# A two-matmul GELU block on one core: the first product wholly in half-row passes, ahead of the second product

## The chip, the core and the metric

The kernel runs on one core of one Trainium2 chip. The metric is device time in microseconds, the median of several runs. The profile used here is one profiled execution of the same kernel on the same kind of chip; all times in it are microseconds from the start of its span unless marked ns.

## The reference

```python
B, S, D, F = 1, 2048, 448, 1792          # all bf16
def reference(x, w1, b1, w2, b2):
    h = jnp.einsum("bsd,df->bsf", x, w1) + b1
    h = _gelu(h)                          # tanh approximation
    return jnp.einsum("bsf,fd->bsd", h, w2) + b2
```

## The kernel before

The 2048 rows of `x` are taken in four chunks of 512 (`SC`), the 1792 hidden columns in 14 tiles of 128 (`NFT`). A "tile" of the first product is one pair (chunk c, hidden tile ft): 128 hidden columns by 512 rows, accumulated in one PSUM bank. There are 56, in the list `order`, and eight banks (`ps`, `NB`).

The contraction of the first product has 448 rows, which is three and a half times 128. `KROW = [0, 128, 256, 320]` cuts both operands into four row blocks; blocks 2 and 3 overlap by 64 rows. A tile is made of three *full* matmuls of 128 rows (`full`, L229) and one *half* matmul of 64 rows (`half`, L237), which uses either the lower or the upper 64 rows of the array. Even tiles take blocks 0, 1, 2 in full and the upper half of block 3; odd tiles take blocks 0, 1, 3 in full and the lower half of block 2 (`SLOTS`, `HALVES`). The halves of two neighbouring tiles use different row halves of the array and so run side by side.

Changing between full and half form is grouped by blocks of eight tiles (`BLOCK`, `FIRST`): the `first` tiles of a block run their full matmuls, then their halves; the `second` tiles begin with their halves and end with their full matmuls. So each of the seven blocks changes form twice. The first block, `opening_block`, goes by row blocks instead of by tiles, because the row blocks of w1 land one after the other (semaphores `sem_w10`, `sem_w1`, and `sem_w1r` for the columns from tile 8 on).

Before the first matmul, 13 dummy matmuls run (L200). Chunk 0 of `x` is loaded in its natural layout and transposed by 16 matmuls with an identity (L214) in six parts (`XPARTS`); each part lies in a bank of its own from `XBANK` on, and VectorE (`d`, L352) or ScalarE (`a`, L336) copies it to `xT_sb`. The bias `b1` is transposed by one small matmul (L205) among them and copied by VectorE (L354). The other three chunks are transposed by their loads (`load_xT`, L164, four transposing DMAs a chunk).

ScalarE evicts each finished tile with GELU and bias (L340) into `g_sb`, in `order`. The second product (`l2`, L317) takes the 128-row stripes of a chunk: 14 matmuls of 448 columns each accumulate in one bank, VectorE adds `b2` (L358), and SP stores the stripe (L183). The last stripe is cut in two column parts.

TensorE's order is the list `schedule`: blocks of the first product, with the second product of a chunk put in as soon as the chunk after it is through the first (chunk 0 after block 3, chunk 1 after block 5, chunks 2 and 3 at the end). `jobs` numbers all bank uses in that order, a bank is taken in turn, and `free` waits until the use eight before has been evicted. SP's queue has the loads in this order: `x` chunk 0, w1, the transposing loads of chunk 1, w2, b2, the transposing loads of chunks 2 and 3, then the stores.

Of the kernel before, what the change touches and what calls it, by code (L numbers as in the profile page):

```python
# [11 lines left out]
def bass_standalone__dense_activation_gelu__prompt_kernel(  # L12
# [10 lines left out]
    P = 128  # L23
    HALF = P // 2
# [17 lines left out]

    BLOCK = 8
    FIRST = [4] + [6] * 6
    W2_PIECES = [(0, 7), (7, 14)]


# [1 line left out]
        ("d", [(0, 0)]), ("a", [(0, 1)]), ("d", [(1, 0)]), ("a", [(1, 1)]),  # L53
        ("d", [(0, 2), (0, 3)]), ("a", [(1, 2), (1, 3)]),
    ]
    XBANK = 1
    NB = 8

    NWARM = 13
# [2 lines left out]
    OCUT = 256  # L62

    order = [(c, ft) for c in range(NSC) for ft in range(NFT)]
    BLOCKS = []
    for i, n in enumerate(FIRST):
        tiles = order[i * BLOCK:(i + 1) * BLOCK]
        BLOCKS.append((tiles[:n], tiles[n:]))
    assert len(BLOCKS) * BLOCK == len(order)

    schedule = []
    done = 0
    for i, (first, second) in enumerate(BLOCKS):
        schedule.append(("l1", i))
        while done < NSC - 2 and (done + 1, NFT - 1) in order[:(i + 1) * BLOCK]:
            schedule.append(("l2", done))
            done += 1
    schedule += [("l2", c) for c in range(done, NSC)]

    outs = [(j, 0, D) for j in range(NST - 1)] + [(NST - 1, 0, OCUT), (NST - 1, OCUT, D)]  # L80

    jobs = []
    for what, c in schedule:
        if what == "l1":
            jobs += [("g", order.index(tile)) for part in BLOCKS[c] for tile in part]
        else:
            jobs += [("o", n) for n, (j, _, _) in enumerate(outs) if j // STC == c]
    number = {job: n for n, job in enumerate(jobs)}  # L90

    with ExitStack() as es:
# [27 lines left out]
        sem_b1T = S_("sem_b1T")  # L120
        sem_b1 = S_("sem_b1")
        sem_l1 = S_("sem_l1")
        sem_g = S_("sem_g")
        sem_l2 = S_("sem_l2")
        sem_osb = S_("sem_osb")
# [11 lines left out]
        def x_part(n, parts):  # L137
            h, k = parts[0]
            to = xT_sb[:, k:k + len(parts), 2 * h * P:2 * (h + 1) * P]
            src = ps[XBANK + n][:, 0:2 * P * len(parts)]  # L140
            return to, src.rearrange("p (k t) -> p k t", k=len(parts))

        def load_w1(eng):
# [26 lines left out]
        @block.sync  # L170
        def _(sp):
            sp.dma_start(xn_sb[:, 0:2, :], x0_view[:, 0:2, :]).then_inc(sem_xn[0], 16)  # L172
            sp.dma_start(xn_sb[:, 2:4, :], x0_view[:, 2:4, :]).then_inc(sem_xn[1], 16)  # L173
            load_w1(sp)
            load_xT(sp, 1)
            for i in range(len(W2_PIECES)):
                load_w2(sp, i)
            sp.dma_start(b2_bc[:, :], b2.partition_broadcast(P)).then_inc(sem_b2, 16)
            for c in range(2, NSC):
                load_xT(sp, c)  # L180
            for j in range(NST - 1):
                sp.wait_ge(sem_osb, j + 1)
                sp.dma_start(out_dram(j), out_sb[:, j, :]).then_inc(sem_od, 16)  # L183
            sp.wait_ge(sem_od, 16 * NST)
# [11 lines left out]
        def _(pe):  # L196
            ones_w = nc.const_aps.tensor(1.0, [P, P], BF16)
            ones_x = nc.const_aps.tensor(1.0, [P, WN], BF16)
            for _i in range(NWARM):
                pe.matmul(ps[0][:, 0:WN], lhsT=ones_w, rhs=ones_x, start=True, stop=True)  # L200
            pe.wait_ge(sem_id, 2)
            for n, (_, parts) in enumerate(XPARTS):
                if n == 2:
                    pe.wait_ge(sem_b1n, 16)
                    pe.matmul(  # L205
                        ps[NB - 1][:, 0:NFT], lhsT=b1n_sb[:, :], rhs=ident[0:NFT, 0:NFT],
                        start=True, stop=True,
                    ).then_inc(sem_b1T, 1)
                for h, k in parts:
                    if (h, k) in ((0, 0), (1, 0)):  # L210
                        pe.wait_ge(sem_xn[h], 16)
                    for t in range(2):
                        col = parts.index((h, k)) * 2 * P + t * P
                        mm = pe.matmul(  # L214
                            ps[XBANK + n][:, col:col + P],
                            lhsT=xn_sb[:, 2 * h + t, KROW[k]:KROW[k] + P],
                            rhs=ident[:, :],
                            start=True, stop=True,
                        )
                mm.then_inc(sem_xtp, 1)  # L220
# [4 lines left out]
                    kind, i = jobs[n]  # L225
                    pe.wait_ge(sem_g if kind == "g" else sem_osb, i + 1)

            def full(c, ft, k, start, stop):
                return pe.matmul(  # L229
                    bank("g", order.index((c, ft)))[:, :],  # L230
                    lhsT=w1_sb[:, k, ft * P:(ft + 1) * P],
                    rhs=xT_sb[:, k, c * SC:(c + 1) * SC],
                    start=start, stop=stop,
                )

            def half(c, ft, k, lo, start, stop):
                return pe.matmul(  # L237
                    bank("g", order.index((c, ft)))[:, :],
                    lhsT=w1_sb[lo:lo + HALF, k, ft * P:(ft + 1) * P],
                    rhs=xT_sb[lo:lo + HALF, k, c * SC:(c + 1) * SC],  # L240
                    start=start, stop=stop,
                )

            SLOTS = ((0, 1, 2), (0, 1, 3))
            HALVES = ((3, HALF), (2, 0))

            def opening_block(first, second):
                first = [ft for _, ft in first]
                second = [ft for _, ft in second]

                fts = first + second
                for n, ft in enumerate(fts):
                    for i, (a, _) in enumerate(W0_PIECES):
                        if ft == a:
                            pe.wait_ge(sem_w10[i], 16)
                    if n == 0:
                        pe.wait_ge(sem_xTd, 2)
                    elif n == NB - 1:
                        pe.wait_ge(sem_b1, 1)
                    elif XPARTS[n - XBANK][0] == "a":  # L260
                        pe.wait_ge(sem_xTa, sum(e == "a" for e, _ in XPARTS[:n - XBANK + 1]))
                    elif n - XBANK >= 4:
                        pe.wait_ge(sem_xTd, sum(e == "d" for e, _ in XPARTS[:n - XBANK + 1]))
                    full(0, ft, 0, True, False)
                pe.wait_ge(sem_w1[1], 16)
                for n, ft in enumerate(fts):
                    full(0, ft, 1, False, False)
                pe.wait_ge(sem_w1[2], 16)
                pe.wait_ge(sem_w1[3], 16)
                for n, ft in enumerate(first):  # L270
                    full(0, ft, SLOTS[n % 2][2], False, False)
                for n, ft in enumerate(first):
                    half(0, ft, *HALVES[n % 2], False, True).then_inc(sem_l1, 1)
                for n, ft in enumerate(second):
                    half(0, ft, *HALVES[n % 2], False, False)
                for n, ft in enumerate(second):
                    full(0, ft, SLOTS[n % 2][2], False, True).then_inc(sem_l1, 1)

            def block_of(first, second):
                for n, (c, ft) in enumerate(first):  # L280
                    if c > 0 and ft == 0:
                        pe.wait_ge(sem_x[c], 16 * NKT)
                    free("g", order.index((c, ft)))
                    for k in SLOTS[n % 2]:
                        full(c, ft, k, k == 0, False)
                for n, (c, ft) in enumerate(first):
                    half(c, ft, *HALVES[n % 2], False, True).then_inc(sem_l1, 1)
                for n, (c, ft) in enumerate(second):
                    if c > 0 and ft == 0:
                        pe.wait_ge(sem_x[c], 16 * NKT)  # L290
                    free("g", order.index((c, ft)))
                for n, (c, ft) in enumerate(second):
                    half(c, ft, *HALVES[n % 2], True, False)
                for n, (c, ft) in enumerate(second):
                    for k in SLOTS[n % 2]:
                        mm = full(c, ft, k, False, k == SLOTS[n % 2][-1])
                    mm.then_inc(sem_l1, 1)

            def l1(i):
                if i == 0:  # L300
                    opening_block(*BLOCKS[i])
                    pe.wait_ge(sem_w1r, 32)
                else:
                    block_of(*BLOCKS[i])

            def l2(c):
                pe.wait_ge(sem_g, NFT * (c + 1))
# [14 lines left out]
                        )  # L322
                    mm.then_inc(sem_l2, 1)

            for what, c in schedule:
                (l1 if what == "l1" else l2)(c)

        @block.scalar
        def _(act):
# [16 lines left out]

        @block.vector
        def _(dve):
            for n, (e, parts) in enumerate(XPARTS):
                if e == "d":  # L350
                    dve.wait_ge(sem_xtp, n + 1)
                    dve.tensor_copy(*x_part(n, parts)).then_inc(sem_xTd, 1)  # L352
            dve.wait_ge(sem_b1T, 1)
            dve.tensor_copy(b1_f[:, :], ps[NB - 1][:, 0:NFT]).then_inc(sem_b1, 1)  # L354
            dve.wait_ge(sem_b2, 16)
            for n, (j, c0, c1) in enumerate(outs):
                dve.wait_ge(sem_l2, n + 1)
# [32 lines left out]
```

## Time and profile before

| | us |
|---|---|
| median of 3 runs | 96.71 (96.46 to 96.75) |
| profiled execution | 96.25 |
| its span | 94.4 |
| TensorE matmuls busy (PE) | 90.5 |
| TensorE weight loads busy (PEld) | 43.8 |
| ScalarE busy (ACT) | 35.9 |
| VectorE busy (DVE) | 11.7 |

The granted clock of TensorE is 1.0 in every stage of the span. The span is the time from the first to the last instruction that the profile has; the profiled execution's own time is 1.85 us longer. Matmuls are pipelined: a matmul of 512 columns is shown with a duration of about 379 ns though the next may start long before it ends, so a pace is read from several matmuls in a row. In the lines, `PE ps L229 x24` in the chain of waits means 24 instructions of line 229 one after the other; `<-` names what ended the idle time before.

### The profile page before, as it was taken

The numbers are of one execution on the slowest core, as the hardware profiler recorded it, in microseconds if no ns is written. First come the engines' busy times: TensorE is split into PE (matmuls) and PEld (weight loads), VectorE is DVE, ScalarE is ACT, GpSimd is POOL, SyncE is SP. The second block draws the span as 40 slices with busy tenths as digits, with TensorE's granted clock in tenths as the row PEclk, the third lists the DMA queues.
The fourth block names the chain that finished last, engine by engine and source line by source line (L and its number), as shares of the span: only waits on it lengthen the run. The fifth ranks groups of instructions, "written<-read, shape, count | busy, mean of one in ns | idle before, by whom it ended". The sixth has DMA issues, their size and how long they took to land.

```text
span 94.4 us, 1159 instructions
## 1 busy us (share of the span) xinstructions
PE 90.5 (96%) x492; PEld 43.8 (46%) x492; DVE 11.7 (12%) x21; ACT 35.9 (38%) x61; POOL 0.7 (1%) x6
## 2 busy tenths in 40 slices
PE   6989999999999999999999999999999999999990
PEld 4724343443443555544344455554345555555670
DVE  0320000000000022220000001222000222222130
ACT  3520595985958910000793990000099000000000
POOL 2000000000000000000000000000000000000000
PEclk9999999999999999999999999999999999999999
DMA  1999999998520010011000001110000110011111
GB/s 36 275 312 280 192 225 350 301 74 166 111 56 0 0 49 28 27 49 49 3 0 0 0 0 49 49 53 24 28 0 0 49 48 16 33 49 56 49 49 49
DMA packets 12385, 7.50 MB, mean 79 GB/s; under 512 B 7004, under 2 KB 11996, under 8 KB 12380
## 3 DMA queue, kind: packets, MB, share of 16 engines
q1 hardware_dynamic: 12208, 7.31, 32.9%
q10 hardware_dynamic: 172, 0.12, 0.4%
q8 instruction: 4, 0.07, 0.3%
q14 instruction: 1, 0.01, 0.0%
HBM read 4.02 MB, written 1.84 MB: 62 GB/s over the span
## 4 chain that ended last, share of the span: by engine, by line
PE 90%; DMA 5%; SPq 2%; DVE 0%; issue 0%
PE ps L317 45%; PE ps L229 38%; PE ps L237 7%; DMA wi_sb<-in_w_dram 5%; SPq L146 1%; SPq L173 0%; SPq L172 0%; DVE out_sb L358 0%
## 5 line engine op out<-in xcount | busy, mean ns | idle before, releaser
L340 ACT ACTIVATE g_sb<-ps,bi_f 128x512 bf16<-128x512 f32 x56 | 33.1, 702 | 34.9 <-PE ps L237 34.9
L317 PE MATMUL ps<-wo_sb,g_sb 128*128 128x448 bf16 (+2 forms) x238 | 42.9, 341 | 0.0
L229 PE MATMUL ps<-xT_sb,wi_sb 128*128 128x512 bf16 x168 | 38.2, 380 | 0.6 <-DMA wi_sb<-in_w_dram 0.4
L317 PEld LDWEIGHTS ps<-wo_sb,g_sb 128*128 128x128 bf16 x238 | 23.1, 98 | 19.7
L229 PEld LDWEIGHTS ps<-xT_sb,wi_sb 128*128 128x128 bf16 x168 | 15.7, 98 | 21.8 <-issue 3.0
L358 DVE TENSOR_TENSOR out_sb<-ps,bo_bc 128x448 bf16<-128x448 f32 (+2 forms) x17 | 10.2, 597 | 76.8 <-PE ps L317 76.8
L237 PE MATMUL ps<-xT_sb,wi_sb 64*128 64x512 bf16 x56 | 7.3, 379 | 0.0
L237 PEld LDWEIGHTS ps<-xT_sb,wi_sb 64*128 64x128 bf16 x56 | 2.2, 94 | 4.6 <-issue 3.0
L200 PE MATMUL ps<-const-bfloat16-1.0 128*128 128x256 bf16 x13 | 2.9, 410 | 0.8 <-PEq L375 0.8
L200 PEld LDWEIGHTS ps<-const-bfloat16-1.0 128*128 128x128 bf16 x13 | 1.8, 140 | 1.5 <-issue 0.7
L352 DVE CAST xT_sb<-ps 128x256 bf16<-128x256 f32 (+1 forms) x3 | 1.4, 510 | 3.8 <-PE ps L214 3.8
L332 ACT ACT_TABLE_LOAD x1 | 1.3, 1283 | 1.4 <-PEq L375 1.4
L336 ACT CAST xT_sb<-ps 128x256 bf16<-128x256 f32 (+1 forms) x3 | 1.3, 443 | 1.1 <-PE ps L214 1.0
L214 PE MATMUL ps<-ident,xn_sb 128*128 128x128 bf16 x16 | 1.2, 220 | 0.0
L214 PEld LDWEIGHTS ps<-ident,xn_sb 128*128 128x128 bf16 x16 | 1.0, 98 | 0.2
L190 POOL TENSOR_SCALAR_AFFINE_SELECT ident<-ident 128x128 bf16<-128x128 bf16 x1 | 0.3, 292 | 0.2 <-POOL ident L188 0.2
L332 ACT ACTIVATE act_junk<-const-float32-0.0 128x8 bf16<-128x8 f32 x1 | 0.2, 208 | 0.0
L188 POOL MEMSET ident<- 128x128 bf16 x1 | 0.2, 204 | 0.3 <-POOLq L375 0.3
L205 PE MATMUL ps<-ident,bin_sb 14*128 14x14 bf16 x1 | 0.2, 177 | 0.0
L354 DVE COPY bi_f<-ps 128x14 f32<-128x14 f32 x1 | 0.2, 161 | 0.0
L205 PEld LDWEIGHTS ps<-ident,bin_sb 14*128 14x128 bf16 x1 | 0.1, 90 | 0.1
L375 POOL MEMSET const-bfloat16-1.0<- 128x1 bf16 x1 | 0.1, 102 | 0.0
(3 smaller groups left out, 0.3 us busy)
## 6 DMA issues: line engine op xcount, KB each, us to landing
out_dram<-out_sb SPq DMA_DIRECT2D x15, 112.0 KB, 1.7
wo_sb<-in_w_dram SPq DMA_DIRECT2D x2, 784.0 KB, 6.5
wi_sb<-in_w_dram SPq DMA_DIRECT2D x3, 256.0 KB, 4.8
wi_sb<-in_w_dram SPq DMA_DIRECT2D x1, 576.0 KB, 6.8
xn_sb<-in_x_dram SPq DMA_DIRECT2D x2, 224.0 KB, 2.6
wi_sb<-in_w_dram SPq DMA_DIRECT2D x2, 128.0 KB, 3.4
wi_sb<-in_w_dram SPq DMA_DIRECT2D x1, 192.0 KB, 6.9
xT_sb<-in_x_dram SPq DMA_TRANSPOSE x12, 5.0
```

The source lines that it names most:

```text
L146: eng.dma_start(w1_sb[:, 0, a * P:b * P], w1[0:P, a * P:b * P]).then_inc(sem_w10[i], 16)
L200: pe.matmul(ps[0][:, 0:WN], lhsT=ones_w, rhs=ones_x, start=True, stop=True)
L205: pe.matmul(ps[NB - 1][:, 0:NFT], lhsT=b1n_sb[:, :], rhs=ident[0:NFT, 0:NFT], start=True, stop=True,).then_inc(sem_b1T, 1)
L214: mm = pe.matmul(ps[XBANK + n][:, col:col + P], lhsT=xn_sb[:, 2 * h + t, KROW[k]:KROW[k] + P], rhs=ident[:, :], start=True, stop=True,)
L229: return pe.matmul(bank("g", order.index((c, ft)))[:, :], lhsT=w1_sb[:, k, ft * P:(ft + 1) * P], rhs=xT_sb[:, k, c * SC:(c + 1) * SC], sta ...
L237: return pe.matmul(bank("g", order.index((c, ft)))[:, :], lhsT=w1_sb[lo:lo + HALF, k, ft * P:(ft + 1) * P], rhs=xT_sb[lo:lo + HALF, k, c * ...
L317: mm = pe.matmul(bank("o", n)[:, 0:c1 - c0], lhsT=g_sb[:, ft, j * P:(j + 1) * P], rhs=w2_sb[:, ft, c0:c1], start=(ft == 0), stop=(ft == NF ...
L332: act.activation(act_junk[:, :], zero, ACT.Gelu_apprx_tanh)
L336: act.copy(*x_part(n, parts)).then_inc(sem_xTa, 1)
L340: act.activation(g_sb[:, ft, c * SC:(c + 1) * SC], bank("g", i)[:, :], ACT.Gelu_apprx_tanh, bias=b1_f[:, ft:ft + 1], scale=1.0,).then_inc( ...
L352: dve.tensor_copy(*x_part(n, parts)).then_inc(sem_xTd, 1)
L358: dve.tensor_tensor(out=out_sb[:, j, c0:c1], in0=bank("o", n)[:, 0:c1 - c0], in1=b2_bc[:, c0:c1], op=ALU.add,).then_inc(sem_osb, 1)
```

## The change

The full matmuls of the first product are gone. Every tile is made of half-row matmuls alone, always two side by side, one in the lower and one in the upper half of the array's rows, for two neighbouring tiles. Two tiles need fourteen half matmuls, that is seven such *steps*. `PHASES` gives them: in the four steps of phase 0 the lower rows serve tile i+1 and the upper rows tile i; in the three steps of phase 1 it is the other way round. The two tiles have different banks, and the bank that a row half writes changes with the phase. Between a phase and the next of the same two tiles, a step waits (`sem_turn`) until the last step of the earlier phase has finished. Outside the opening, steps go by four tiles (`QUAD`): phase 0 of two tiles, phase 0 of the next two, then phase 1 of each.

The opening (`OPEN`) has 27 steps of the first eight tiles in three parts, one for what needs row block 0 of w1 alone, one after row block 1 has landed, one after blocks 2 and 3. The 28th step is put behind the first phase of tiles 8 and 9.

All 56 tiles now come before the second product; `schedule` and the blocks are gone. On SP's queue the transposing loads of chunks 2 and 3 go ahead of w2 and b2. The small matmul of `b1` goes ahead of the transposes and uses bank 0, its copy goes to the head of VectorE's stream, and the six transposed parts lie in banks 1, 2, 3, 4, 6 and 7.

```diff
-    BLOCK = 8
-    FIRST = [4] + [6] * 6
+    PHASES = (((0, 0), (1, 1), (2, 2), (3, 3)), ((0, 0), (1, 1), (2, 3)))
+    OPEN = (
+        ((0, 0, 0), (1, 0, 0), (2, 0, 0), (0, 1, 0), (1, 1, 0), (3, 0, 0), (2, 1, 0)),
+        ((0, 1, 1), (1, 1, 1), (3, 1, 0), (2, 1, 1), (0, 0, 1), (1, 0, 1), (3, 1, 1)),
+        ((0, 0, 2), (0, 0, 3), (1, 0, 2), (1, 0, 3), (0, 1, 2), (2, 0, 1), (1, 1, 2), (2, 0, 2),
+         (2, 0, 3), (3, 0, 1), (3, 0, 2), (3, 0, 3), (2, 1, 2)),
+    )
+    OPENING = 8
+    QUAD = 4
...
-    XBANK = 1
+    XBANK = [1, 2, 3, 4, 6, 7]
...
-    BLOCKS = []
...
-    schedule += [("l2", c) for c in range(done, NSC)]
+    steps = [(2 * j, h, m) for part in OPEN for j, h, m in part]
+    N_OPEN = [sum(len(part) for part in OPEN[:n]) for n in range(len(OPEN) + 1)]
+    def phase(i, h):
+        return [(i, h, m) for m in range(len(PHASES[h]))]
+    for i in range(OPENING, len(order), QUAD):
+        steps += phase(i, 0)
+        if i == OPENING:
+            steps.append((OPENING - 2, 1, len(PHASES[1]) - 1))
+        steps += phase(i + 2, 0) + phase(i, 1) + phase(i + 2, 1)
+    ahead = {}
+    turn = []
+    for n, (i, h, m) in enumerate(steps):
+        before = ahead.get(i)
+        turn.append(before if before is not None and steps[before][1] != h else None)
+        ahead[i] = n
+    turned = sorted(n for n in turn if n is not None)
...
+    jobs = [("g", i) for i in range(len(order))] + [("o", n) for n in range(len(outs))]
...
             load_xT(sp, 1)
+            for c in range(2, NSC):
+                load_xT(sp, c)
             for i in range(len(W2_PIECES)):
                 load_w2(sp, i)
             sp.dma_start(b2_bc[:, :], b2.partition_broadcast(P)).then_inc(sem_b2, 16)
-            for c in range(2, NSC):
-                load_xT(sp, c)
...
             pe.wait_ge(sem_id, 2)
+            pe.wait_ge(sem_b1n, 16)
+            pe.matmul(
+                ps[0][:, 0:NFT], lhsT=b1n_sb[:, :], rhs=ident[0:NFT, 0:NFT], start=True, stop=True,
+            ).then_inc(sem_b1T, 1)
...
+            def opening_waits(n, i):
+                if n == N_OPEN[1]:
+                    pe.wait_ge(sem_w1[1], 16)
+                if n == N_OPEN[2]:
+                    pe.wait_ge(sem_w1[2], 16)
+                    pe.wait_ge(sem_w1[3], 16)
+                if n < N_OPEN[1] and steps[n][1] == 0:
+                    for p, (a, _) in enumerate(W0_PIECES):
+                        if i == a:
+                            pe.wait_ge(sem_w10[p], 16)
+                    for t in (i, i + 1):
+                        if t == 0:
+                            pe.wait_ge(sem_b1, 1)
+                            pe.wait_ge(sem_xTd, 2)
...
+            def l1():
+                for n, (i, h, m) in enumerate(steps):
+                    if n < N_OPEN[-1]:
+                        opening_waits(n, i)
+                    elif h == 0 and m == 0:
+                        if n == N_OPEN[-1]:
+                            pe.wait_ge(sem_w1r, 32)
+                        for t in (i, i + 1):
+                            c, ft = order[t]
+                            if c > 0 and ft == 0:
+                                pe.wait_ge(sem_x[c], 16 * NKT)
+                            free("g", t)
+                    if turn[n] is not None:
+                        pe.wait_ge(sem_turn, turned.index(turn[n]) + 1)
+                    lower, upper = PHASES[h][m]
+                    first = h == 0 and m == 0
+                    last = h == 1 and m == len(PHASES[1]) - 1
+                    for lo, tile, k in ((0, i + 1 - h, lower), (HALF, i + h, upper)):
+                        mm = half(tile, k, lo, first, last)
+                        if last:
+                            mm.then_inc(sem_l1, 1)
+                    if n in turned:
+                        mm.then_inc(sem_turn, 1)
...
-            for what, c in schedule:
-                (l1 if what == "l1" else l2)(c)
+            l1()
+            for c in range(NSC):
+                l2(c)
...
+            dve.wait_ge(sem_b1T, 1)
+            dve.tensor_copy(b1_f[:, :], ps[0][:, 0:NFT]).then_inc(sem_b1, 1)
             for n, (e, parts) in enumerate(XPARTS):
...
-            dve.wait_ge(sem_b1T, 1)
-            dve.tensor_copy(b1_f[:, :], ps[NB - 1][:, 0:NFT]).then_inc(sem_b1, 1)
```

More of the change, by code (lines that the diff above doesn't have):

```diff
@@ L64, in bass_standalone__dense_activation_gelu__prompt_kernel @@
     order = [(c, ft) for c in range(NSC) for ft in range(NFT)]
-    BLOCKS = []
[L66 to L77, printed above, removed]
-    schedule += [("l2", c) for c in range(done, NSC)]
-    outs = [(j, 0, D) for j in range(NST - 1)] + [(NST - 1, 0, OCUT), (NST - 1, OCUT, D)]
-    jobs = []
-    for what, c in schedule:
[L86 to L89, printed above, removed]
+    steps = [(2 * j, h, m) for part in OPEN for j, h, m in part]
[7 more added lines that the diff above has]
+        steps += phase(i + 2, 0) + phase(i, 1) + phase(i + 2, 1)
+    assert len(set(steps)) == len(steps) == len(order) // 2 * 7
+    ahead = {}
[5 more added lines that the diff above has]
+    turned = sorted(n for n in turn if n is not None)
+    outs = [(j, 0, D) for j in range(NST - 1)] + [(NST - 1, 0, OCUT), (NST - 1, OCUT, D)]
+    jobs = [("g", i) for i in range(len(order))] + [("o", n) for n in range(len(outs))]
     number = {job: n for n, job in enumerate(jobs)}
@@ L122, in bass_standalone__dense_activation_gelu__prompt_kernel @@
         sem_l1 = S_("sem_l1")
+        sem_turn = S_("sem_turn")
         sem_g = S_("sem_g")
@@ L139, in x_part @@
             to = xT_sb[:, k:k + len(parts), 2 * h * P:2 * (h + 1) * P]
-            src = ps[XBANK + n][:, 0:2 * P * len(parts)]
+            src = ps[XBANK[n]][:, 0:2 * P * len(parts)]
             return to, src.rearrange("p (k t) -> p k t", k=len(parts))
@@ L201, in _ @@
             pe.wait_ge(sem_id, 2)
+            pe.wait_ge(sem_b1n, 16)
+            pe.matmul(
+                ps[0][:, 0:NFT], lhsT=b1n_sb[:, :], rhs=ident[0:NFT, 0:NFT], start=True, stop=True,
+            ).then_inc(sem_b1T, 1)
             for n, (_, parts) in enumerate(XPARTS):
[L203 to L208, printed above, removed]
                 for h, k in parts:
@@ L214, in _ @@
                         mm = pe.matmul(
-                            ps[XBANK + n][:, col:col + P],
+                            ps[XBANK[n]][:, col:col + P],
                             lhsT=xn_sb[:, 2 * h + t, KROW[k]:KROW[k] + P],
@@ L226, in free, with half @@
                     pe.wait_ge(sem_g if kind == "g" else sem_osb, i + 1)
-            def full(c, ft, k, start, stop):
+            def half(i, k, lo, start, stop):
+                c, ft = order[i]
                 return pe.matmul(
[L230 to L238, printed above, removed]
+                    bank("g", i)[:, :],
                     lhsT=w1_sb[lo:lo + HALF, k, ft * P:(ft + 1) * P],
@@ L242, in half @@
                 )
[L244 to L304, printed above, removed]
+            def opening_waits(n, i):
[12 more added lines that the diff above has]
+                            pe.wait_ge(sem_xTd, 2)
+                        elif t in XBANK:
+                            x = XBANK.index(t)
+                            e = XPARTS[x][0]
+                            pe.wait_ge(
+                                sem_xTd if e == "d" else sem_xTa,
+                                sum(f == e for f, _ in XPARTS[:x + 1]),
+                            )
@@ L323, in l2 @@
                     mm.then_inc(sem_l2, 1)
-            for what, c in schedule:
-                (l1 if what == "l1" else l2)(c)
+            l1()
+            for c in range(NSC):
+                l2(c)
         @block.scalar
```

## The prediction, made before the change was run

> **What bounds the kernel now.** I read the totals first, then the chain of waits, then the groups, and last the timeline around one change of matmul form. The totals:
>
> ```profile
> PE 90.5 (96%) x492; PEld 43.8 (46%) x492; DVE 11.7 (12%) x21; ACT 35.9 (38%) x61; POOL 0.7 (1%) x6
> ```
>
> TensorE is busy in nearly the whole span and no other engine passes 38%. So the time is the number of passes through TensorE times their pace, plus what is lost between them. The chain of waits (start, length, what) shows both:
>
> ```profile
> 2.60 4.58 DMA wi_sb<-in_w_dram
> 7.18 0.05 issue
> 7.22 2.76 PE ps L229 x12
> 9.99 0.97 PE ps L237 x8
> 10.96 4.86 PE ps L229 x22
> 15.81 0.97 PE ps L237 x8
> 16.78 5.29 PE ps L229 x24
> ...
> 30.70 10.59 PE ps L317 x56
> 41.29 3.89 PE ps L229 x18
> ...
> 70.65 21.24 PE ps L317 x126
> 91.89 0.02 issue
> 91.91 0.36 DVE out_sb L358
> ```
>
> L229 is a full matmul of the first product, L237 a half-row one (two run side by side), L317 the second product. From 7.22 to 91.89 nothing but TensorE stands in the chain: no DMA, no gelu, no eviction. The 18 full ones at 41.29 give the undisturbed pace, 3.89/18 = 0.216 us a pass. Against that, 24 full ones that follow halves take 5.29, not 5.18: 0.11 too many. Eight halves are four pairs and take 0.97, not 0.864: again 0.106. So each change of form, full to half or half to full, costs about 0.107 us. The second product has none: 10.59/56 = 0.189 for 448 columns.
>
> Inside the pairs (timeline, about one microsecond of it):
>
> ```profile
> 15.97 0.81 PE L237 MATMUL ps<-xT_sb,wi_sb 64*128 64x512 bf16 x6
> 16.19 0.10 PEld L237 LDWEIGHTS ps<-xT_sb,wi_sb 64*128 64x128 bf16 x2
> ```
>
> Three pairs take 0.81, of which the last one's own duration is 0.376: (0.81-0.376)/2 = 0.217 between pairs. Both weight loads of the next pair start with the running pair and are done 0.10 later, over 0.1 us before they are needed. The opening in the same view gives the lag from matmul to gelu, and the gelus' group their pace:
>
> ```profile
> 9.92 1.04 PE L237 MATMUL ps<-xT_sb,wi_sb 64*128 64x512 bf16 x8
> 10.41 4.15 ACT L340 ACTIVATE g_sb<-ps,bi_f 128x512 bf16<-128x512 f32 x7 [5.02 <-PE ps L237]
> ```
>
> ```profile
> L340 ACT ACTIVATE g_sb<-ps,bi_f 128x512 bf16<-128x512 f32 x56 | 33.1, 702 | 34.9 <-PE ps L237 34.9
> ```
>
> The lag is 0.49 (9.92 to 10.41), and a stream of gelus advances by 33.1/56 = 0.591 each, the last one taking 0.70.
>
> **The passes.** A tile of the first product now costs three full passes and half of a pair, 3.5 in all; afterwards seven pair steps serve two tiles, 3.5 again. So 56 tiles are 196 slots of 0.216 before and after, and the second product keeps its 238 matmuls. Nothing is won in arithmetic, only between passes.
>
> **What is removed.** Seven blocks with two changes of form each: 14 x 0.107 = 1.50 us. As a test of the account: from 7.22 the pieces of the first product last 42.25. They hold 160 full passes and 28 pairs, 188 x 0.2158 = 40.57, plus 1.50, plus 0.16 because the first piece ends with a whole modelled duration (0.379) instead of a step. That is 42.23, so no other loss is hiding there.
>
> **What is added in changes of form.** Transposes to half passes: TensorE stands still before the first pass anyway (idle 0.4, waiting for wi_sb), so nothing. Half passes to the second product: one, 0.107. Net 13 x 0.107 = 1.39 won.
>
> The Trainium skill speaks against long runs of half passes: "TensorE: Matmul & The Clock Gate", Part 3, says that a weight load overlaps running matmuls only where its row group differs from theirs. In a run of pairs both row groups are always busy. The row above has the loads beside the running pair, and so the row decides. By the rule each of some 189 slots would grow by about one load (0.094 us in the trace), an estimate of 17.8 us, and the kernel would need some 114 us.
>
> **The opening.** The first product's start is set by DMAs. Before, eight full k=0 passes run from 5.17 until w1's second row block lands (7.18). Afterwards only seven pair steps (OPEN's first part) stand ahead of that wait, so 21 instead of 20 slots of the opening's 28 come after 7.22: +0.216. The seven end at 5.17+7x0.216 = 6.69, so two turn waits there and the second column piece (2.1+3.4 = 5.5, needed at 5.6) are covered by the 0.5 left.
>
> Then four covers get thin, each against its row (issue and landing from the lines of w1's loads):
> - w1's fourth row block: issued 3.5, 5.0 to landing, 8.55; with 0.05 release and 0.09 weight load 8.69. Needed at 7.23+7x0.216 = 8.74.
> - The rest of w1: issued 4.50, 6.9 to landing, 11.4; with the same, 11.54. Needed at 7.23+20x0.216 = 11.55 (before: about 11.8).
> - Tiles 8 and 9 take the banks of 0 and 1, nine slots (1.94) after the last pair of these starts. The lag is 0.49, two gelus take 0.59+0.70, a load 0.09: 1.87.
> - Tiles 10 and 11 take those of 2 and 3: 14 slots (3.02) after the same start, against 0.49+3x0.59+0.70+0.09 = 3.05.
>
> They share one shift: being late once relaxes the next. I take 0.10 for all; the bounds are 0 and about 0.5 (a landing that much later).
>
> The bias matmul moves ahead of the transposes, and its copy (0.16) to the head of DVE. Its bracket in TensorE's stream cost about 0.2 before and now delays DVE's first transposed part by 0.2 to 0.25. Two parts are needed for the first pass; they were done at about 4.68, so now at 4.9. Cover: the wi_sb landing that lets PE start at 5.17. Without it, 0.25.
>
> **The turn waits.** At each change of role, 36 in all, a step waits on the semaphore of an earlier step of the same two tiles. Distances from the step list: 4 times three slots, 17 times four, 11 times five, 4 times more. Behind the wait stands everything on TensorE, since its queue is in order. The trace has no wait of TensorE on itself. The nearest is the lag from matmul start to gelu start, 0.49; with a weight load 0.58. Three slots are 0.65, four 0.86, so the wait is over before its step is due. Bounds: 0 (a gain is excluded, since a wait cannot shorten passes), and a full drain like a change of form, 0.107. I take 0, by the 0.49 row.
>
> **Steady bank waits.** Four tiles take 14 slots, 3.02 us; four gelus 4x0.591 = 2.36. A bank is taken again after 28 slots, 6.0 us, so no gelu is late.
>
> **SP's queue.** Eight transposing loads move past the two w2 loads and b2. They occupy SP 13.01 us before (from 13.11); now they start at 11.3 and end at about 24.3, so the third chunk's should land near 22 and the fourth's near 28, needed at slots 98 and 144: 26.9 and 36.8. The second chunk's order is unchanged: last issue 9.8, landed about 13.3, needed at 15.6. w2 goes out near 24.5 and lands near 31 (6.5 each), b2 likewise (7.0), needed at 48. The cost is nothing; without cover it would be TensorE's wait one for one. The first outputs now come after 48, at the pace that the last eight tiles have already (one per 2.65 against 0.62 of DVE).
>
> **Sum.** Span 94.4 - 1.39 + 0.216 + 0.10 = 93.3. The profiled execution took 96.25, 1.85 outside its span; it becomes 95.2. The median, 96.71, lies 0.46 above it; with the same 1.07 taken off it becomes 95.6. The spread of the three runs (0.29, or 0.3%) is about what a measurement of this kernel can tell from no change.
>
> **Rivals.**
> 1. *Forecast*, 0.67: changes of form vanish, waits stay covered. Own range 95.2 to 96.0 (covers 0 to 0.5, medians within 0.15).
> 2. *The opening takes the gain back*, 0.15: the w1 landings have stragglers (4.6, 4.8, 5.0 us for three equal loads) and their slack has gone from 0.3 to 0.02, so a lag of 0.5 to 1.0 now counts whole: 96.0 to 96.6. For: the four thin covers. Against: before, the same landing at 7.18 already sets the start, and a general delay moves both kernels.
> 3. *The turn waits drain TensorE*, 0.13, slower: 34 exposed turns x 0.107 = 3.6; 95.6+3.6 = 99.2. It decides from 1.07/34 = 0.03 us a turn on. For: the load after a wait can't be pulled ahead until the semaphore arrives. Against: 0.58 is under even three slots.
> 4. *Pairs don't hold their pace*, 0.05: the trace has at most four pairs in a row, with twice the instructions per slot. Each 0.006 a slot eats the gain (189 x 0.006 = 1.1); 0.02 gives 99.4. Against: the transposes (L214, 128 columns) pass a load and a matmul every 0.056, so four instructions in 0.216 are no strain.
>
> **How the numbers follow.** Faster: 0.67 and two thirds of case 2, 0.77. Same: the rest of case 2 and a little of 3, 0.06. Slower: 0.17. The range 95.1 to 96.8 holds cases 1 and 2; outside lie cases 3 and 4 and a little below.
>
> **What would show it.** In the profile after, no L229 group; the half-row line with 392 matmuls, its pieces in the chain near 0.216 per two matmuls, one unbroken stretch of about 40.9 us from 7.2 to 48.2, and the second product in one stretch of 42.4 us. PE's idle time before the half-row line, other than for wi_sb, should be under 0.2. If turn waits cost, PE waits for itself 30 times or more; if pairs are slow, the stretch grows evenly in every window. A stretch much over 42 makes the forecast wrong.

## The result, and the profile after

| | before | after |
|---|---|---|
| median of 6 runs | 96.63 us | 95.27 us (95.04 to 95.47) |
| ratio to before, 95% interval | | 0.9875 (0.985 to 0.990) |
| profiled execution, its span | 96.25, 94.4 | 95.47, 93.7 |

The change makes the kernel faster by 1.25%, 1.21 us of the 96.63 (0.97 to 1.45); the two medians in the table lie 1.36 apart, within that interval. The profiled execution of after is the slowest of its runs, so its span shows less of the gain than the median does.

The totals of the changed kernel:

```profile
PE 90.3 (96%) x660; PEld 48.3 (52%) x660; DVE 11.9 (13%) x21; ACT 36.5 (39%) x61; POOL 0.7 (1%) x6
```

There are 168 more matmuls and as many more weight loads, and yet TensorE is busy for about the same time. The chain of waits (start, length, what) says where the change lies:

```profile
3.83 1.82 PE ps L223 x16
5.65 42.94 PE ps L239 x386
48.59 42.53 PE ps L304 x238
91.11 0.02 issue
91.14 0.36 DVE out_sb L346
```

L239 is the half-row matmul, L304 the second product. The alternating full and half pieces of before have become one, and the three pieces of the second product too: 42.53 against 10.59+10.59+21.24 = 42.42 before, where the 0.11 more is the one change of form that is left (the kernel with the order alone, below, has none there, and its second product takes 42.42 in one stretch). Whether the pairs keep their pace can be read from a long window of the timeline, past the opening:

```profile
13.01 35.36 PE L239 MATMUL ps<-xT_sb,wi_sb 64*128 64x512 bf16 x326
```

These are 163 pairs without a break: (35.36-0.376)/162 = 0.2160 us from pair to pair. Four pairs in a row was the most that the trace of before could show, and 163 run at the same pace. The waits that TensorE still has, and ScalarE's:

```profile
ACT g_sb L328 <- PE ps L239: 10.4, 12, 4.2
...
PEld ps L239 <- PE ps L239: 0.4, 2, 0.3
...
PEld ps L239 <- DMA wi_sb<-in_w_dram: 0.4, 2, 0.2
...
PEld ps L239 <- ACT g_sb L328: 0.3, 1, 0.3
```

The columns are the total, the times and the longest. With 36 turn waits in the program, weight loads waited for a matmul of the first product twice, both in the opening. The one wait for a gelu is tiles 10 and 11 taking their banks (a step of 0.236 instead of 0.216, so 0.02 lost). These are idle times of the loads; the matmuls hide most of them.

The opening is the only place where this profile is worse than the earlier one. The group of the transposing matmuls, before and after:

```profile
L214 PE MATMUL ps<-ident,xn_sb 128*128 128x128 bf16 x16 | 1.2, 220 | 0.0
```

```profile
L223 PE MATMUL ps<-ident,xn_sb 128*128 128x128 bf16 x16 | 1.9, 312 | 0.0
```

The start of the first product before, with the loads that wait for row block 1 of w1 (7.22), and the first weight loads after:

```profile
5.17 4.81 PE L229 MATMUL ps<-xT_sb,wi_sb 128*128 128x512 bf16 x20 [0.40 <-DMA wi_sb<-in_w_dram]
...
7.22 2.27 PEld L229 LDWEIGHTS ps<-xT_sb,wi_sb 128*128 128x128 bf16 x12 [0.64 <-DMA wi_sb<-in_w_dram]
```

```profile
5.60 0.21 PEld L239 LDWEIGHTS ps<-xT_sb,wi_sb 64*128 64x128 bf16 x4 [0.22 <-DMA wi_sb<-in_w_dram]
6.01 0.15 PEld L239 LDWEIGHTS ps<-xT_sb,wi_sb 64*128 64x128 bf16 x2 [0.20 <-DMA wi_sb<-in_w_dram]
6.43 0.15 PEld L239 LDWEIGHTS ps<-xT_sb,wi_sb 64*128 64x128 bf16 x2 [0.28 <-PE ps L239]
6.73 4.84 PEld L239 LDWEIGHTS ps<-xT_sb,wi_sb 64*128 64x128 bf16 x46 [0.15 <-PE ps L239]
```

A transposing matmul takes 312 ns in the mean, 220 in the profile of before. The loads come with the steps, and the first four steps lie 0.41, 0.42 and 0.30 apart instead of 0.216, together 0.48 more. From 6.73 on the pace is the usual one. The lines name waits for these loads, but the waits are not what spaces the steps: in the third profile of the changed kernel the same steps with the same waits start at the same time, and the loads of seven steps follow each other at the usual pace:

```profile
5.60 1.19 PEld L239 LDWEIGHTS ps<-xT_sb,wi_sb 64*128 64x128 bf16 x14 [0.54 <-DMA wi_sb<-in_w_dram]
```

In the profile of after the instructions themselves are slow there: loads of 0.15 instead of 0.10, and half matmuls of up to 0.63 instead of 0.376. So TensorE ran at about half its pace until about 6.6 us in this execution. The text below calls that a low clock; it is read from these durations, since the windows view gives a granted clock of 1.00 there too. The first step started at 5.60, when the first column piece of w1 had landed, against 5.17 in the profile of before.

### The profile page after: what moved, and what is told of

It reads as the page before. It is cut to its first block, busy times and chain, and to the rows that moved or that the text cites. A ratio compares the mean times of both kernels' runs of the same rounds, so it can differ in the third digit from the quotient of the medians.

```text
span 93.7 us, 1513 instructions
## 1 busy us (share of the span) xinstructions
PE 90.3 (96%) x660; PEld 48.3 (52%) x660; DVE 11.9 (13%) x21; ACT 36.5 (39%) x61; POOL 0.7 (1%) x6
## 4 chain that ended last, share of the span: by engine, by line
PE 96%; DVE 0%; issue 0%
PE ps L239 46%; PE ps L304 45%; PE ps L211 3%; PE ps L223 2%; DVE out_sb L346 0%; PE ps L214 0%
## 5 line engine op out<-in xcount | busy, mean ns | idle before, releaser
L239 PE MATMUL ps<-xT_sb,wi_sb 64*128 64x512 bf16 x392 | 43.0, 379 | 0.0
L304 PE MATMUL ps<-wo_sb,g_sb 128*128 128x448 bf16 (+2 forms) x238 | 42.6, 342 | 0.0
L328 ACT ACTIVATE g_sb<-ps,bi_f 128x512 bf16<-128x512 f32 x56 | 33.7, 694 | 10.4 <-PE ps L239 10.4
L304 PEld LDWEIGHTS ps<-wo_sb,g_sb 128*128 128x128 bf16 x238 | 23.0, 98 | 19.8 <-issue 0.4
L239 PEld LDWEIGHTS ps<-xT_sb,wi_sb 64*128 64x128 bf16 x392 | 21.8, 95 | 20.9 <-PE ps L239 0.4
L223 PE MATMUL ps<-ident,xn_sb 128*128 128x128 bf16 x16 | 1.9, 312 | 0.0
L223 PEld LDWEIGHTS ps<-ident,xn_sb 128*128 128x128 bf16 x16 | 1.6, 146 | 0.0
```

The source lines that it names most:

```text
L223: mm = pe.matmul(ps[XBANK[n]][:, col:col + P], lhsT=xn_sb[:, 2 * h + t, KROW[k]:KROW[k] + P], rhs=ident[:, :], start=True, stop=True,)
L239: return pe.matmul(bank("g", i)[:, :], lhsT=w1_sb[lo:lo + HALF, k, ft * P:(ft + 1) * P], rhs=xT_sb[lo:lo + HALF, k, c * SC:(c + 1) * SC], ...
L304: mm = pe.matmul(bank("o", n)[:, 0:c1 - c0], lhsT=g_sb[:, ft, j * P:(j + 1) * P], rhs=w2_sb[:, ft, c0:c1], start=(ft == 0), stop=(ft == NF ...
L328: act.activation(g_sb[:, ft, c * SC:(c + 1) * SC], bank("g", i)[:, :], ACT.Gelu_apprx_tanh, bias=b1_f[:, ft:ft + 1], scale=1.0,).then_inc( ...
```

## The experiments

The theory: a change between full and half form costs 0.107 us each, and the gain is the 13 that are gone, less what the opening gives back. The rivals: the gain comes from the order (all tiles ahead of the second product, or the loads' new order); turn waits or the opening cost something that hides a larger gain. Every ratio is to the kernel before, run on the same chip; the changed kernel's own is 0.9875 to 0.989 in three comparisons. Code cuts are marked with three dots.

**The order alone.** The old blocks, but with the new order of products and loads.

```diff
-        while done < NSC - 2 and (done + 1, NFT - 1) in order[:(i + 1) * BLOCK]:
+        while done < 0 and (done + 1, NFT - 1) in order[:(i + 1) * BLOCK]:
...
             load_xT(sp, 1)
+            for c in range(2, NSC):
+                load_xT(sp, c)
...
-            for c in range(2, NSC):
-                load_xT(sp, c)
```

> The kernel before with its blocks and full matmuls kept, but all 56 tiles ahead of the second product and the transposing loads of chunks 2 and 3 ahead of w2, as in the changed kernel. Theory (the gain is changes of form, 0.107 us each): still 14 changes, so no difference from before, 96.6 within 0.3. Rival (the order of the products or of the loads brings the gain): about 95.3.

Measured: 96.41 us against 96.36, ratio 1.0005 (0.9983 to 1.0028). The order brings nothing and costs nothing, to within 0.3 us: moving eight transposing loads past w2 was hidden, as the prediction had it. The rival falls.

**Two insertions.** The changed kernel with chunk 0's and chunk 1's second product put back between the tiles, and the old order of loads.

```diff
+    AT = {32: [0, 1, 2, 3], 48: [4, 5, 6, 7]}
...
             load_xT(sp, 1)
-            for c in range(2, NSC):
-                load_xT(sp, c)
...
                 for n, (i, h, m) in enumerate(steps):
+                    if h == 0 and m == 0 and i in AT:
+                        for s in AT[i]:
+                            l2_stripe(s)
...
```

> The changed kernel with half-row steps kept, but the loads in the old order and the second product of chunks 0 and 1 put back where it was (after 32 and after 48 tiles). Theory: two insertions are four more changes of form, 4 x 0.107 = 0.43 on top of the changed kernel's 95.3, so 95.7. Rival (order brings the gain): 96.6. No difference from 95.3 would say that a change of form between the two products costs less than one inside the first.

Measured: 95.58 us, ratio 0.9914 (0.989 to 0.9938), 0.38 us more than the changed kernel's 0.9875; four changes at 0.107 are 0.43. The two intervals overlap, so the medians alone would not prove the price. Its chain shows it: each of the inserted stretches takes 10.70, 0.11 more than the 10.59 of before, which had full matmuls on both sides, and the 56 steps between them take 12.19 where 56x0.2158 is 12.08.

```profile
30.39 10.70 PE ps L312 x56
41.09 12.19 PE ps L243 x112
53.29 10.70 PE ps L312 x56
```

**Eight insertions.** The same with one stripe at a time after every fourth tile from tile 24 on.

```diff
-    AT = {32: [0, 1, 2, 3], 48: [4, 5, 6, 7]}
+    AT = {24: [0], 28: [1], 32: [2], 36: [3], 40: [4], 44: [5], 48: [6], 52: [7]}
```

> As the kernel with two insertions, but eight single stripes of the second product, each put between two groups of four tiles: 16 more changes of form than the changed kernel. Theory: 16 x 0.107 = 1.71 on top of 95.3, so 97.0, slower than before; in the trace each change shows a step of 0.31 instead of 0.216. Rival (order or the turn waits decide): within 0.5 of the kernel with two insertions.

Measured: 96.92 us, ratio 1.0049 (1.0024 to 1.0074), slower than before. Against the two insertions it has twelve changes more and 0.0135 x 96.36 = 1.30 us more: 0.108 each, give or take 0.03 by the two intervals. Half passes and all, the whole gain is gone once the form changes often enough. The chain of waits of this kernel is the account itself:

```profile
26.93 3.13 PE ps L243 x28
30.06 2.75 PE ps L312 x14
32.82 3.13 PE ps L243 x28
35.95 2.75 PE ps L312 x14
```

28 halves are 14 steps, 14x0.2158 = 3.02, and the piece takes 3.13; 14 matmuls of the second product are 14x0.189 = 2.65, and the piece takes 2.75. Each has one change of form in it, 0.11 and 0.10.

**Blocks of four in the kernel before.** The dose from the other side, without any half-row scheme.

```diff
-    BLOCK = 8
-    FIRST = [4] + [6] * 6
+    SIZES = [(8, 4)] + [(4, 2)] * 12
...
```

> The kernel before with blocks of four tiles after the first block (two tiles begin in full, two in halves), so 26 changes of form instead of 14, nothing else. Theory: 12 x 0.107 = 1.28 more than before, 97.9. If a change of form costs only where it meets another wait, under 97.2.

Measured: 97.78 us, ratio 1.0136 (1.0109 to 1.0162). Twelve more changes cost 0.0136 x 96.36 = 1.31 us, 0.109 each (give or take 0.02), with nothing else moved. The chain:

```profile
23.35 0.54 PE ps L240 x4
23.89 2.69 PE ps L232 x12
```

Two pairs, 0.432, take 0.54; twelve full passes, 2.59, take 2.69. So three kernels that add changes, and the change itself that takes them out, agree on the price.

**The turn waits.** The changed kernel with the step behind a turn wait moved nearer to the step that it waits for: the distance falls from four slots to three, two and one as the kernel goes on.

```diff
-        steps += phase(i + 2, 0) + phase(i, 1) + phase(i + 2, 1)
+        a, b = phase(i, 1), phase(i + 2, 1)
+        lead = 3 if i == OPENING else 2 if i < 28 else 1 if i < 44 else 0
+        steps += phase(i + 2, 0) + a[:lead] + b[:1] + a[lead:] + b[1:]
```

> The changed kernel with the first step after a turn wait moved nearer to the step that it waits for: distance three slots in the groups of four from tile 12 to 27 (four turns), two slots in those from 28 to 43 (four turns), one slot in those from 44 on (three turns); the other tile pair's steps fill in behind. Theory (a step can start some 0.43 after the start of the one it waits for, plus up to 0.09 of weight load): three slots (0.65) cost nothing, two (0.43) up to 0.1 each, one (0.216) 0.2 to 0.3 each, in all 0.6 to 1.3 us more than the changed kernel. Rival (a turn wait costs a drain of about 0.107 whatever its distance): the three-slot turns show it already, and the changed kernel too.

Measured: 96.19 us, ratio 0.9964 (0.9941 to 0.9986) beside the changed kernel's 0.9877 (0.9846 to 0.9907) on the same chip: 0.84 us more. The timeline over the three distances (start, length, engine, line, count):

```profile
12.98 15.50 PE L241 MATMUL ps<-xT_sb,wi_sb 64*128 64x512 bf16 x142
```

```profile
28.54 12.12 PE L241 MATMUL ps<-xT_sb,wi_sb 64*128 64x512 bf16 x110
```

```profile
36.80 11.05 PE L241 MATMUL ps<-xT_sb,wi_sb 64*128 64x512 bf16 x94
```

```profile
40.72 2.70 PEld L241 LDWEIGHTS ps<-xT_sb,wi_sb 64*128 64x128 bf16 x28 [0.56 <-PE ps L241]
43.98 2.70 PEld L241 LDWEIGHTS ps<-xT_sb,wi_sb 64*128 64x128 bf16 x28 [0.56 <-PE ps L241]
47.24 0.33 PEld L241 LDWEIGHTS ps<-xT_sb,wi_sb 64*128 64x128 bf16 x6 [0.56 <-PE ps L241]
```

Three slots: (15.50-0.376)/70 = 0.2161 from pair to pair over 71 pairs, so the waits cost nothing. Two slots: (12.12-0.376)/54 = 0.2175, 0.08 lost in three whole turns and the tail of a fourth, about 0.024 each. One slot: (11.05-0.376)/46 = 0.2320 in a window with three such turns and one of two slots: 0.74 lost, about 0.24 for each of the three, and there the weight loads stand idle for 0.56. The steps fall 0.444 us apart instead of 0.216. So a step can start 0.44 us after the start of the step it waits for, weight load included (0.43+0.024 by the two-slot turns). The 0.84 lies between the expected 0.6 and 1.3, nearer the lower end because the load adds almost nothing to the wait. The changed kernel's shortest distance outside its opening is four slots, 0.86.

**Eight steps first.** The eighth step of row block 0 ahead of the wait for row block 1.

```diff
-        ((0, 0, 0), (1, 0, 0), (2, 0, 0), (0, 1, 0), (1, 1, 0), (3, 0, 0), (2, 1, 0)),
-        ((0, 1, 1), (1, 1, 1), (3, 1, 0), (2, 1, 1), (0, 0, 1), (1, 0, 1), (3, 1, 1)),
+        ((0, 0, 0), (1, 0, 0), (2, 0, 0), (0, 1, 0), (1, 1, 0), (3, 0, 0), (2, 1, 0),
+         (3, 1, 0)),
+        ((0, 1, 1), (1, 1, 1), (2, 1, 1), (0, 0, 1), (1, 0, 1), (3, 1, 1)),
```

> The changed kernel with the eighth step of row block 0 (tiles 6 and 7, phase 1) put ahead of the wait for row block 1, so that eight steps instead of seven stand before that landing. Theory of the prediction (the landing sets the start, one slot lies needlessly behind it): 0.2 faster than the changed kernel, about 95.1. Rival (in most executions the first steps run at a low clock and the landing is over by then, as in the changed kernel's profile): no difference.

Measured: 95.11 us, ratio 0.9858 (0.9834 to 0.9881), beside 0.9877 (0.9846 to 0.9907) of the changed kernel. Run again beside the changed kernel:

> The kernel with eight steps ahead of the wait for row block 1, once more, beside the changed kernel on one chip, since the first comparison left 0.18 us between them with intervals that overlap. If the landing of row block 1 is a wall in most executions: 0.2 faster than the changed kernel. If it is a wall in some only, as its landing at 6.6 to 7.2 in the profiles against a first part that ends at 6.9 to 7.2 suggests: under 0.1.

> The changed kernel as the reference of that comparison: ratio to before 0.9875 within 0.003.

Measured: 0.987 (0.9837 to 0.9903) against 0.989 (0.9854 to 0.9926). Twice it is 0.002 faster, 0.2 us, and both times the intervals overlap, so the question stays open. Its ratios are the lowest of those tried, and it is clearly faster than before, but not shown to be faster than the changed kernel. The profiles leave little for it to win: with seven steps ahead, the eighth step was never more than 0.03 late (see below), and moved ahead it stands two slots behind the step that it waits for, which costs 0.02 by the turn waits above.

**The bias matmul back behind the first two parts.** VectorE's copy of it moves back too.

```diff
-            pe.wait_ge(sem_b1n, 16)
-            pe.matmul(
-                ps[0][:, 0:NFT], lhsT=b1n_sb[:, :], rhs=ident[0:NFT, 0:NFT], start=True, stop=True,
-            ).then_inc(sem_b1T, 1)
             for n, (_, parts) in enumerate(XPARTS):
+                if n == 2:
+                    pe.wait_ge(sem_b1n, 16)
+                    pe.matmul(
+                        ps[0][:, 0:NFT], lhsT=b1n_sb[:, :], rhs=ident[0:NFT, 0:NFT], start=True, stop=True,
+                    ).then_inc(sem_b1T, 1)
...
```

> The changed kernel with the bias matmul back behind the first two transposed parts and its copy behind VectorE's second part. Rival on the opening (the early bias matmul makes TensorE stand still between the dummy matmuls and the transposes, the clock is granted later, and that costs the 0.4 that the profile of the changed kernel shows): 0.2 to 0.4 faster, and the clock granted near 3.5 us in its profile. Theory (the grant's time is chance): no difference in the median.

Measured: 95.07 us, ratio 0.9876 (0.9844 to 0.9908), the same as the changed kernel beside it. In its profile the transposes take 277 ns in the mean, and the first steps come at the usual pace.

> The changed kernel once more beside the three others, as their reference and for a second profile. Both theories: 95.3 within 0.2; the profile tells whether the clock is again granted late in the opening.

The changed kernel again: 95.24 us, 0.9877, its transposes at 313 ns and its first three steps 0.40 and 0.38 apart, late as in the first profile. The low clock in the opening is not the change's doing, though. The kernel with the order alone has the old opening and the old place of the bias matmul, and in its profile the transposes are as slow:

```profile
L214 PE MATMUL ps<-ident,xn_sb 128*128 128x128 bf16 x16 | 2.1, 312 | 0.0
```

Of the twelve profiles five show 220 ns (before, two insertions, eight insertions, turn distance, eight first the second time), four 312 or 313 (after twice, the order alone, blocks of four), and three lie between. Both openings are in both sets.

## Why the prediction held

It was 95.6 with a range of 95.1 to 96.8; 95.27 was measured, 0.3 lower. The forecast gain of 1.07 stands against 1.21 (0.97 to 1.45).

- *The changes of form*, 13 x 0.107 = 1.39: right. Two measured doses give 0.108 and 0.109, each within 0.03, and the pieces of the chains 0.10 to 0.11. The price was already in the trace of before, as the same 0.106 left over in pieces of 8 and of 24 matmuls.
- *The pace of long runs of pairs* (rival 4): the row of before held, 0.216 over 163 pairs. The sentence of the Trainium skill that was weighed against it ("TensorE: Matmul & The Clock Gate", Part 3, weight loads overlap running matmuls only where the row group differs) does not hold here; its estimate of 17.8 us would have been seen. The full passes of before already spoke against it, 0.216 apart with a load of 98 ns for each. The same Part also lets a load run ahead when it goes to the background weight buffer, and that fits both rows.
- *The turn waits* (rival 3): taken at 0 by the 0.49 us from matmul to gelu, and at 0 they are. The runs put TensorE's own distance at 0.44 to 0.46, a little under that row, and show what would have happened: 0.24 a turn at one slot.
- *SP's queue and the order*: nothing, as forecast. Here it was measured without the half passes.
- *The opening*, +0.216 and +0.10: the size is not contradicted (1.39 less 1.21 leaves 0.18, between -0.06 and 0.42), but the cause of the 0.216 was not what the prediction named. It took row block 1's landing at 7.18 as a wall behind seven steps (three of them, not two, have a turn wait). In the profile of after the eighth step was due at 7.6, after that block had landed at about 7.1, and nothing waited for it. In none of the seven profiles with seven steps ahead of that wait was the eighth step more than 0.03 late. Of the three profiles with the old opening only that of before shows the wall: its ninth pass was due at 6.90 and started at 7.22. So the wall belonged to one execution with the earliest start of all twelve (5.17; the others 5.37 to 5.72) and a late landing. That the sum came out even so is in part luck: the term is smaller than the 0.24 by which the measured gain is uncertain.
- *What the opening cost instead*, in the two profiles: the start came 0.43 later (+0.43), the steps at the low clock +0.48, the bank wait of tiles 10 and 11 +0.02, and the wall was gone, -0.31. With the 1.39 taken off that makes -0.77; by the chains the last addition ends at 92.27 before and at 91.50 after, 0.77 earlier. The account closes, but the start and the clock of the opening vary from one execution to the next.
- *Four thin covers*: the bank wait took its 0.02 in every profile of the changed kernel. w1's fourth row block came late in four of the nine profiles with the new opening. It was worst with two insertions, where the block's landing ends the wait in the chain:

```profile
3.54 5.37 DMA wi_sb<-in_w_dram
8.91 0.14 issue
9.04 21.35 PE ps L243 x196
```

  The fifteenth step, the first that needs the block, started 0.47 late there. In the third profile of the changed kernel its loads come only at 8.83, after an idle stretch:

```profile
7.08 1.22 PEld L239 LDWEIGHTS ps<-xT_sb,wi_sb 64*128 64x128 bf16 x14 [0.29 <-DMA wi_sb<-in_w_dram]
8.83 2.52 PEld L239 LDWEIGHTS ps<-xT_sb,wi_sb 64*128 64x128 bf16 x26 [0.53 <-issue]
```

  Their idle time is 0.53 there, against 0.29 in the line above, where the step was on time: 0.22 lost. The other two (eight first the second time, eight insertions) lost 0.16 and 0.12. Over the nine profiles that is 0.11 in the mean, and 0.13 with the bank wait, beside the 0.10 that the prediction took for all four covers. Rival 2 is real, then, but a few tenths and not in every execution; its 96.0 to 96.6 did not come about.
- *What was to be seen*: no group of full matmuls in the first product, 392 halves, one unbroken stretch, and the second product in 42.5. All of it is there. The stretch is longer than said, 42.9 against 40.9, because it runs from 5.65 and not from a wall at 7.2. Its end, 48.6 instead of 48.2, is later by the opening. The prediction's sign of being wrong, a stretch "much over 42", was therefore not a safe one: it fits only a stretch that begins at the wall, and 42.9 comes near it although the pairs kept their pace.

## What to carry to other kernels

A cost between instructions is found by dividing pieces of the chain of waits by their counts and comparing pieces of different length: what is left over per piece is the price of its border. When a new wait is added, compare the distance in slots with the lag that the trace shows for the nearest pair of engines, and measure the curve once with the distance reduced; here three slots cost nothing, two are the edge, and one costs 0.24 a turn. A landing that ends a wait in one profile need not be a wall in the median, so a term of the sum that rests on it deserves a second profile.

## What the runs showed of the hardware

- A change between 128-row and 64-row matmuls costs about 0.107 us in either direction (0.10 to 0.11 by the pieces of the chains, 0.108 and 0.109 by two doses), whether full passes of 512 columns or of 448 stand beside it.
- TensorE can wait by semaphore on its own result and go on 0.44 to 0.46 us later, from start to start of 512-column half matmuls.
- The low clock in the opening comes and goes between executions of kernels with the same opening: 128-column matmuls at 220 ns in one profile, 312 in another, after the same 13 dummy matmuls. "TensorE: Matmul & The Clock Gate", Part 1, says that the window which releases the clock runs freely and does not start with the kernel; these profiles fit that, but none shows the window itself. The windows view still gives a granted clock of 1.00 there, so it was the durations that showed it: transposing matmuls twice as far apart (0.107 instead of 0.056), steps 0.42 instead of 0.216.
